# Reordering the opening of a tuned FFT and GEGLU kernel: warm matmuls in a row, tables ahead of the folds, and one load held back

## The chip, the cores and the metric

One core of one Trainium2 chip. The metric is the device time of one execution in microseconds (us); medians and ranges of several executions are given. A traced execution has a "span", from its first to its last recorded instruction; the time of the same execution is about 2 us longer (620.6 against 622.64 for the kernel before). All positions in a trace are us from the start of the span.

## The reference

Shortened; numpy and `erf` are imported.

```python
def _attn_ref(x):                      # x: 8 x 3008 x 256, float32
    X = np.fft.fft(x, axis=1)
    X = np.fft.fft(X, axis=2)
    return X.real.astype(np.float32)

def _moe_ref(x, w_gate, w_val, w_out): # x: 24064 x 256, d_ff 1536
    g = x @ w_gate
    gelu = 0.5 * g * (1.0 + erf(g / sqrt(2)))
    val = x @ w_val
    return (gelu * val @ w_out).astype(np.float32)

# reference: _moe_ref(_attn_ref(x).reshape(24064, 256), ...)
```

## The kernel before

The Fourier transform along the sequence is done by matmuls on "folded" input (sums and differences of a row and its mirror), and the one along the channels is merged into the weights: CW times the raw weights gives W_sb, with a "minus" copy of some of it. Per batch there are five folds (PIECES), a first transform stage (`s1`, evicted into A_sb), a channel stage (`ch`, into Z_sb) and a twiddle stage (`tp_e`, `tp_o`, `tp_y`) that yields the E and O halves of the feed-forward's input; `tp_y` makes the row of the border channel (EB_sb). The feed-forward then runs in 288 equal steps, called slots: 36 for each batch. In each slot TensorE does a gate, a value and an output part, and `plan()` lays the transform of the coming batches into the slots, on TensorE (`fill`) and on GpSimd (`pool`).

Batch 0 has nothing to hide behind. `opening()` does it: issue the loads, build tables, warm TensorE's clock with matmuls on a zero tile, fold, transform. A line `# ...` stands for what is left out.

```python
    def make_w(i, f0, n, parts=(0, 1), engine="A", m_at=None, tag="dft"):
        # ... matmuls CW x w_raw into ps, eviction into W_sb on `engine` ...
                def minus():
                    dst, src = W["gv"[i], "M"][:, f0 : f0 + n], ps[:, m - n : m]
                    if engine == "A":
                        nc.scalar.activation(dst, src, AF.Copy, scale=keep2)
                    else:
                        nc.vector.tensor_scalar(dst, src, keep2, None, op0=ALU.mult)

    def opening():
        # ... x of batch 0 (part by SyncE), weights, x of batch 1, output weights: issued by GpSimd ...
        vec_consts(); vec_fills()
        warm(7)
        g_phases(); t_columns(); t_phases()
        # ... twiddle and CW tables on ScalarE and VectorE ...
        warm(6)
        fold_piece(9, 4)
        s1(0, 2, 0)(); s1(0, 2, 1)()
        warm(8)
        fold_piece(13, 4)
        # ... remaining folds and s1 ...
        make_w(0, 0, 256, m_at=minus, tag="o")()
        ch(0, 0)(); ch(0, 1, "V")()
        # ...
    def plan():
        for s, f in (
                (0, make_w(0, 256, 256)), (0, make_w(1, 256, 256, engine="V")),
                (1, make_w(1, 512, 512, (1,))), (2, make_w(0, 512, 512, (0,), "V")),
                # ... slots 3 to 5 ...
                (6, make_w(0, 1024, 512, (1,))), (6, make_yw()), (7, make_w(1, 1024, 512, (0,), "V"))):
            at(fill, s, f)
        for k, s in ((0, 8), (1, 9), (2, 9)):            # x of batch 2, on SyncE's queue
            at(fill, s, lambda k=k: load_part(2, k, (load_forward,)))
        # ...
            if b == 1:                                   # batch 1's folds on GpSimd, by slot
                slot_of = [4, 4, 5, 5, 6, 6, 7, 7, 8, 8, 9, 13, 13, 14, 15, 15, 16, 17, 17, 18]
```

Slot 8 in the program does not keep the load of x for batch 2 from starting much earlier: SyncE has nothing else to do, and the load goes out as soon as its buffer, which holds batch 0's x, has been read by the last fold. That is at 15.31 us.

Of the kernel before, what the change touches and what calls it, by code (L numbers as in the profile page):

```python
# [12 lines left out]
ALU = mybir.AluOpType  # L13
# [5 lines left out]
def _sub(base: bass.AP, free_pattern, free_offset, part_start=0, part_num=None):  # L19
    p_step, p_count = base.ap[0]  # L20
    if part_num is None:
        part_num = p_count - part_start
    pat = [[p_step, part_num]] + [list(x) for x in free_pattern]
    off = base.offset + part_start * p_step + free_offset
    return ap_replace(base, ap=pat, offset=off)
# [3 lines left out]
def kernel(  # L29
# [234 lines left out]
    def reduced(d, r, f):  # L264
        nc.vector.tensor_scalar(r, f, MAGIC, None, op0=ALU.add)
        nc.vector.scalar_tensor_tensor(d, r, MAGIC, f, op0=ALU.subtract, op1=ALU.subtract)
# [97 lines left out]

    def cw_phases():
        nc.scalar.activation(cf[:, 0:128], row_c, AF.Copy, scale=col_n0)
        reduced(cd[:, 0:128], cr[:, 0:128], cf[:, 0:128])

    def cw_magnitude():
# [22 lines left out]
    def t_columns():  # L392
        ps = psum("v")
        for i in range(5):
            nc.tensor.matmul(ps[:, i : i + 1], par[:, i, :], one[:, int(i == 0) : int(i == 0) + 1], start=True, stop=True)  # L395
        nc.scalar.activation(parc, ps[:, 0:5], AF.Copy)

    def t_phases():
        k1 = _sub(row_t, [[1, K1]], 0)
        for i in range(2):  # L400
            nc.scalar.activation(
                tf[:, i * K1 : (i + 1) * K1], k1, AF.Identity, scale=parc[:, 0:1], bias=parc[:, 1 + i : 2 + i])

    def t_reduced():
        reduced(td[:, :], tr[:, :], tf[:, :])
# [33 lines left out]

    V3_TO = 1024  # L440

    def make_w(i, f0, n, parts=(0, 1), engine="A", m_at=None, tag="dft"):

        def run():
            ps = psum(tag)
            for k, part in enumerate(parts):
                for half in range(2):
                    nc.tensor.matmul(  # L448
                        ps[:, k * n : (k + 1) * n], CW[:, part, half, :], w_raw[:, i, half, f0 : f0 + n],
                        start=half == 0, stop=half == 1)  # L450
            m = n * len(parts)
            dst = _sub(W_sb, [[F, len(parts)], [1, n]], (2 * i + parts[0]) * F + f0)
            if engine == "A":
                nc.scalar.activation(dst, ps[:, :m], AF.Copy)
            else:
                nc.vector.tensor_copy(dst, ps[:, :m])  # L456
            if 1 in parts and (i == 0 or f0 < V3_TO):
                def minus():
                    if i and f0 == 0:
                        W["v", "M"] = work([128, V3_TO], BF16, "osb", 3, "w_minus")[:, :]  # L460
                    dst, src = W["gv"[i], "M"][:, f0 : f0 + n], ps[:, m - n : m]
                    if engine == "A":
                        nc.scalar.activation(dst, src, AF.Copy, scale=keep2)
                    else:
                        nc.vector.tensor_scalar(dst, src, keep2, None, op0=ALU.mult)

                if m_at is None:
                    minus()
                else:
                    m_at.append(minus)  # L470
        return run
# [44 lines left out]
                nc.vector.tensor_copy(dst, src)  # L516
        return run

    def ch(b, pp, engine="A"):

        def run():
            st = state(b)
            A = st["A"]
            if "Z" not in st:
                st["Z"] = Z_tile()
            ps = ps_any(b)
            for q in range(2):
                k = 2 * (2 * pp + q)
                for g in range(2):
                    nc.tensor.matmul(  # L530
                        ps[:, q * C : (q + 1) * C], _sub(A, [[1, 128]], g * NK * K1 + k * K1), II[:, g, :, :],
                        start=g == 0, stop=g == 1)
            dst = _sub(st["Z"], [[1, 512]], pp * 512)
            if engine == "A":
                nc.scalar.activation(dst, ps[:, :], AF.Copy)
            else:
                nc.vector.tensor_copy(dst, ps[:, :])
        return run

    def s1t(b, jg, half):  # L540
# [252 lines left out]
    def opening():  # L793
# [20 lines left out]
        cast_forward(1, 0, 9)  # L814
        for j0, nj in ((5, 4), (1, 4), (0, 1)):
            cast_mirror(1, j0, nj)
        for q in range(2):
            load_wo(q)
        idle = gelu_tile()[:, 0, :]
        nc.vector.memset(one[:, 0:1], 1.0)  # L820
        sin_table()
# [11 lines left out]

        vec_consts()
        vec_fills()
        warm(7)
        g_phases()
        t_columns()
        t_phases()
        g_rows(9, 7)  # L840
        t_reduced()
        vec_consts2()
        identities()
        cw_phases()
        g_ends()
        cw_magnitude()
        vec_fills2()
        g_rows(1, 8)
        t_sin()
        cw_sin()  # L850
        gelu_table()
        warm(6)
        fold_piece(9, 4)
        s1(0, 2, 0)()
        s1(0, 2, 1)()
        warm(8)
        fold_piece(13, 4)
        cw_rest()
        fold_piece(5, 4)
        s1(0, 1, 0)()  # L860
        s1(0, 1, 1)()
        warm(2)
        fold_piece(0, 1)
        s1(0, 3, 0)()
        s1(0, 3, 1)()
        fold_piece(1, 4)
        t_write()
        s1(0, 0, 0)()
        s1(0, 0, 1, "V")()
        minus = []  # L870
        make_w(0, 0, 256, m_at=minus, tag="o")()
        ch(0, 0)()
        ch(0, 1, "V")()
        make_w(1, 0, 256, m_at=minus, tag="g")()
        tp_e(0, 0, 0, "V", tag="v")()
        tp_e(0, 0, 1, "A", tag="v")()
        minus[0]()
        minus[1]()

    def behind_first_gate():  # L880
        tp_y(0, 0)()

    NS = NG * NFC

    def plan():
# [8 lines left out]
            e = "A" if gi == 1 else "V"  # L894
            early += [ch(0, 2 * gi), ch(0, 2 * gi + 1, e), tp_e(0, gi), tp_o(0, gi, e), tp_y(0, gi)]
        for s, f in (
                (0, make_w(0, 256, 256)), (0, make_w(1, 256, 256, engine="V")), 
                (1, make_w(1, 512, 512, (1,))), (2, make_w(0, 512, 512, (0,), "V")), 
                (3, make_w(0, 512, 512, (1,))), (3, make_w(1, 512, 512, (0,), "V")),
                (4, make_w(1, 1024, 512, (1,), "V")), (5, make_w(0, 1024, 512, (0,), "V")),   # L900
                (6, make_w(0, 1024, 512, (1,))), (6, make_yw()), (7, make_w(1, 1024, 512, (0,), "V"))):
            at(fill, s, f)
        for i, f in enumerate(early):
            at(fill, (7, 8, 9, 10, 11, 12, 13, 14, 15, 16)[i], f)

        for k, s in ((0, 8), (1, 9), (2, 9)):
            at(fill, s, lambda k=k: load_part(2, k, (load_forward,)))
        for k, s in ((0, 18), (1, 19), (2, 19)):
# [16 lines left out]
        for b in range(1, B):  # L925
# [2 lines left out]
            for j0, nj in PIECES:  # L928
                ops += fold_ops(b, j0, nj, nc.gpsimd)
            per = len(ops) // 5  # L930
            first, n = {2: (s0 - 10, 27), 3: (s0 - 19, 30)}.get(b, (s0 - 22, 32))
            slot_of = [first + i * n // len(ops) for i in range(len(ops))]
            if b == 1:
                slot_of = [4, 4, 5, 5, 6, 6, 7, 7, 8, 8, 9, 13, 13, 14, 15, 15, 16, 17, 17, 18]
            for s, f in zip(slot_of, ops):
# [24 lines left out]
    def feed():  # L960
# [11 lines left out]
        for i, (parts, fc) in enumerate(blocks):  # L972
# [2 lines left out]
                pend = list(works[i // NFC - 1])  # L975
            two = sooner.pop(i, []) if i <= NFC + 2 else [pend.pop(0) for _ in range(2) if pend]
            parts["G"][fc]()
            if i == 0:
                behind_first_gate()
            if before:  # L980
                before[0]["g"][before[1]]()
            parts["V"][fc]()
# [49 lines left out]
```

## Time and profile before

| | kernel before |
|---|---|
| time, median of 3 (range) | 624.27 us (622.54 to 624.77) |
| time of the profiled execution | 622.64 us, near the low end |
| TensorE busy | 611.3 of 620.6 us |
| O half of the first gate on TensorE | 20.39 us |
| last value weights issued / landed | 13.64 / 27.3 us |
| batch 1's first fold on GpSimd | 31.21 us |

The lines that carry the opening are in the prediction. The columns of its timelines: start, duration, engine, line, operation, tiles, and in brackets the idle time ahead and what ended it.

The DMA view of 20 to 25 us, by queue: packets, MB and share. q1 carries SyncE's loads, q0 those of GpSimd.

```profile
q1 hardware_dynamic: 135, 0.97, 82.9%
q0 software_dynamic: 136, 0.19, 21.0%
```

The two queues take turns: 135 packets and 136. But a packet of SyncE's load of x for batch 2 carries 7.2 KB on average (0.97 MB over 135) and one of GpSimd's queue 1.4 KB. "DMA: Bandwidth & Descriptors", Queues, rings and completion order, says this: each engine goes round the queues it has work for, a packet at a time. The trace agrees on equal turns.

### The profile page before, as it was taken

The page shows a single profiled execution, that of the slowest core. Times are in us where ns is not written, and L with a number is a line of the kernel's source. Part 1 is how long each engine was busy: PE and PEld are TensorE (multiplying, and loading weights), DVE is VectorE, ACT ScalarE, POOL GpSimd, SP SyncE. Part 2 cuts the span into 40 slices and gives each one's busy share as a digit, 9 for nine tenths or more (in the row PEclk, how much of TensorE's full clock was granted, in tenths as well). Part 3 has the DMA queues.
Part 4 walks back from the last instruction along what each step waited for, and adds up shares of the span by engine and source line. Part 5 has one row for each costly group of instructions (what it writes and reads, how often), then busy time and mean ns, then how long its engine had stood idle before and what let it go on. Part 6 is the DMA issues. An engine that isn't in the chain of part 4 may idle for free.

```text
span 620.6 us, 12788 instructions
## 1 busy us (share of the span) xinstructions
PE 611.3 (98%) x4229; PEld 406.8 (66%) x4229; DVE 576.7 (93%) x939; ACT 425.8 (69%) x827; POOL 504.6 (81%) x510
## 2 busy tenths in 40 slices
PE   8999999999999999999999999999999999999997
PEld 4456666666666666666666666666666666666666
DVE  7689998999999999999999999999999999999992
ACT  5878667776767677667767677766776667666661
POOL 8399899999997999879997899969987555555651
PEclk9999999999999999999999999999999999999999
DMA  9951826545363353631654335543122321221123
GB/s 184 232 91 30 241 62 152 134 123 158 107 158 90 103 142 97 171 103 46 168 126 114 107 88 129 136 109 92 48 65 72 95 65 48 65 52 41 41 52 82
DMA packets 52464, 65.40 MB, mean 105 GB/s; under 512 B 7627, under 2 KB 47276, under 8 KB 50002
## 3 DMA queue, kind: packets, MB, share of 16 engines
q1 hardware_dynamic: 45470, 49.03, 30.1%
q0 software_dynamic: 6608, 15.29, 11.4%
q8 instruction: 33, 0.54, 0.4%
q10 hardware_dynamic: 320, 0.26, 0.2%
q14 instruction: 33, 0.27, 0.2%
HBM read 39.65 MB, written 30.17 MB: 112 GB/s over the span
## 4 chain that ended last, share of the span: by engine, by line
PE 93%; DVE 2%; DMA 2%; ACT 1%; SPq 1%; issue 1%; POOL 0%; DVEq 0%; ACTq 0%; POOLq 0%
PE ps_o L757 38%; PE ps_g L668 29%; PE ps_v L668 19%; PE ps_dft L549 2%; PE ps_dft L585 2%; PE ps_o L828 1%; SPq L662 1%; DMA out_dram<-out_sb 1%; DMA EB_sb<-yrow 1%; PE ps_dft L448 0%; PE ps_v L395 0%; ACT A_sb L514 0%; PE ps_dft L530 0%; DVE h_sb L724 0%; ACT gelu_sb L684 0%
## 5 line engine op out<-in xcount | busy, mean ns | idle before, releaser
L732 POOL TENSOR_TENSOR h_sb<-gelu_sb,v_sb 128x512 bf16<-128x512 bf16 (+1 forms) x280 | 319.4, 1145 | 88.6 <-DVE v_sb L730 83.0
L757 PE MATMUL ps_o<-Wo_sb,h_sb 128*128 128x256 bf16 (+1 forms) x2232 | 334.6, 273 | 0.6 <-POOL h_sb L732 0.6
L757 PEld LDWEIGHTS <-h_sb 128*128 128x128 bf16 (+1 forms) x2304 | 228.7, 100 | 111.7 <-POOL h_sb L732 1.9
L684 ACT ACTIVATE gelu_sb<-ps_g 128x512 bf16<-128x512 f32 (+1 forms) x288 | 169.6, 589 | 98.7 <-PE ps_g L668 88.9
L712 DVE SCALAR_TENSOR_TENSOR ve_sb<-EB_sb,yw,ps_v 128x512 f32<-128x512 bf16 (+1 forms) x280 | 206.3, 737 | 21.2 <-PE ps_v L668 18.0
L668 PEld LDWEIGHTS <-W_sb 128*128 128x128 bf16 x1440 | 138.0, 98 | 80.8 <-issue 3.2
L728 DVE TENSOR_TENSOR h_sb<-gelu_sb,ps_v 128x512 bf16<-128x512 bf16 (+1 forms) x280 | 189.7, 678 | 1.1 <-ACT gelu_sb L693 0.7
L730 DVE SCALAR_TENSOR_TENSOR v_sb<-ve_sb,ps_v 128x512 f32<-128x512 f32 (+1 forms) x280 | 187.4, 669 | 0.0
L668 PE MATMUL ps_g<-O_sb,W_sb 128*128 128x512 bf16 (+1 forms) x576 | 169.1, 375 | 0.1
L693 ACT ACTIVATE gelu_sb<-ps_g 128x512 bf16<-128x512 f32 (+1 forms) x288 | 169.2, 587 | 0.0
L668 PE MATMUL ps_g<-E_sb,W_sb 128*128 128x512 bf16 (+1 forms) x288 | 108.1, 375 | 0.7 <-ACT gelu_sb L693 0.5
L668 PE MATMUL ps_v<-E_sb,W_sb 128*128 128x512 bf16 (+1 forms) x288 | 108.1, 375 | 0.6 <-DVE W_sb L456 0.5
L668 PE MATMUL ps_v<-O_sb,W_sb 128*128 128x512 bf16 (+1 forms) x288 | 108.1, 375 | 0.0
L777 ACT ACTIVATE out_sb<-ps_o 128x512 f32<-128x512 f32 x92 | 55.0, 597 | 35.0 <-PE ps_o L757 34.7
L229 POOL TENSOR_TENSOR eo_sb<-ab_sb 94x512 bf16<-94x512 f32 (+1 forms) x70 | 77.6, 1111 | 0.4
L552 ACT ACTIVATE S_sb<-ps_dft 96x512 bf16<-96x512 f32 x56 | 33.0, 589 | 18.9 <-PE ps_dft L549 18.9
L225 POOL TENSOR_TENSOR ab_sb<-x_raw,x_raw 94x508 f32<-94x508 f32 (+1 forms) x30 | 33.0, 1100 | 0.0
L222 POOL TENSOR_TENSOR ab_sb<-x_raw,x_raw 94x508 f32<-94x508 f32 (+1 forms) x30 | 32.9, 1098 | 0.0
L549 PE MATMUL ps_dft<-eo_sb,G 94*96 94x256 bf16 x119 | 22.3, 273 | 0.0
L595 ACT ACTIVATE E_sb<-ps_dft 128x512 bf16<-128x512 f32 (+1 forms) x23 | 13.5, 588 | 8.7 <-PE ps_dft L585 8.7
L163 POOL DMA_INDIRECT x_raw<-in_x_dram,idx x18 | 17.0, 946 | 2.9 <-issue 1.1
L595 ACT ACTIVATE O_sb<-ps_dft 128x512 bf16<-128x512 f32 (+1 forms) x22 | 12.9, 588 | 7.3 <-PE ps_dft L585 6.7
(151 smaller groups left out, 207.3 us busy)
## 6 DMA issues: line engine op xcount, KB each, us to landing
out_dram<-out_sb SPq DMA_DIRECT2D x364, 64.0 KB
x_raw<-in_x_dram SPq DMA_DIRECT2D x10, 768.0 KB
Z_sb<-z SPq DMA_DIRECT2D x7, 768.0 KB
z<-S_sb SPq DMA_DIRECT2D x7, 576.0 KB
EB_sb<-yrow SPq DMA_DIRECT2D x6, 376.2 KB
z<-S_sb SPq DMA_DIRECT2D x7, 192.0 KB
x_raw<-in_x_dram SPq DMA_DIRECT2D x2, 640.0 KB
x_stage<-in_x_dram SPq DMA_DIRECT2D x1, 768.0 KB
```

The source lines that it names most:

```text
L225: eng.tensor_tensor(ab(1, 1, up), mir(1, up), fwd(255, down), op=ALU.add)
L229: eng.tensor_tensor(_sub(eo, [[C, nj], [1, 128]], j0 * C + g * 128), ab(0, 0, [[1, 128]]), ab(1, 0, [[1, 128]]), op=op)
L549: nc.tensor.matmul(ps[:96, q * C : (q + 1) * C], G[:, j, :], _sub(eo, [[1, C]], j * C), start=(j == js[0]), stop=(j == js[-1]))
L668: nc.tensor.matmul(ps[:, :n], W[nm, part][:, fs], src, start=start, stop=stop, **kw)
L684: nc.scalar.activation(gl[:, 0, :n], pg[:, :n], AF.Gelu)
L693: nc.scalar.activation(_sub(gl, [[-1, n]], TOK + n - 1), pg[:, :n], AF.Gelu)
L712: nc.vector.scalar_tensor_tensor(ve[:, :n], EB_bufs[b][:, c0 : c0 + n], yw[:, fc : fc + 1], pv[:, :n], op0=ALU.mult, op1=ALU.add)
L728: nc.vector.tensor_tensor(st["h"][:, fc, 0, :n], gl[:, 0, :n], pv[:, :n], op=ALU.mult)
L730: nc.vector.scalar_tensor_tensor(_sub(vv, [[-1, n]], n - 1), ve[:, :n], 2.0, pv[:, :n], op0=ALU.mult, op1=ALU.subtract)
L732: nc.gpsimd.tensor_tensor(st["h"][:, fc, 1, :n], gl[:, 1, :n], vv[:, :n], op=ALU.mult)
L757: nc.tensor.matmul(pso[:m, half], st["h"][:, fc, sign, h0 : h0 + m], Wo_sb[:, fc, :], start=(fc == 0 and not (first and sign)), stop=(fc = ...
L777: nc.scalar.activation(_sub(osb, [[1, 2 * C]], 0, part_num=m), pso[:m, :], AF.Copy)
```

## The change

The diff is cut at "...". Its intent: fill VectorE's idle time with all tables so that the folds start when x lands; release TensorE's clock with 16 warm matmuls in a row; start ScalarE's evictions of A earlier (and write Z in halves of 256 columns on both engines); take minus weights off ScalarE and VectorE in the first slots; and keep x of batch 2 from loading until a row that is made in slot 6 has been written.

```diff
-    def make_w(i, f0, n, parts=(0, 1), engine="A", m_at=None, tag="dft"):
+    def make_w(i, f0, n, parts=(0, 1), engine="A", m_at=None, m_engine=None, tag="dft"):
...
+                    if m_engine == "P":
+                        nc.gpsimd.tensor_scalar(dst, W["gv"[i], "O"][:, f0 : f0 + n], keep2, None, op0=ALU.mult)
...
-        warm(7)
+        warm(16)
+        cw_phases()
         g_phases()
-        t_columns()
-        t_phases()
+        columns = t_columns()
         g_rows(9, 7)
-        t_reduced()
+        cw_reduced()
+        vec_fills2()
         vec_consts2()
         identities()
-        cw_phases()
+        cw_magnitude()
+        cw_sin()
+        cw_rest()
         g_ends()
...
-        warm(6)
+        t_phases(columns)
         fold_piece(9, 4)
+        first, second = fold_ops(0, 13, 4, nc.vector)
+        first()
+        t_reduced()
+        second()
         s1(0, 2, 0)()
         s1(0, 2, 1)()
+        t_sin()
+        gelu_table()
         warm(8)
...
-        ch(0, 0)()
-        ch(0, 1, "V")()
+        ch(0, 0, qs=(0,))()
...
+        ch(0, 0, "V", qs=(1,))()
+        ch(0, 1, qs=(0,))()
+        ch(0, 1, "V", qs=(1,))()
...
-                (0, make_w(0, 256, 256)), (0, make_w(1, 256, 256, engine="V")), 
-                (1, make_w(1, 512, 512, (1,))), (2, make_w(0, 512, 512, (0,), "V")), 
+                (0, make_w(0, 256, 256, m_engine="P")), (0, make_w(1, 256, 256, engine="V", m_engine="P")),
+                (1, make_w(1, 512, 512, (1,), m_engine="P")), (1, lambda: load_wo(0)), (1, lambda: load_wo(1)),
...
-                (6, make_w(0, 1024, 512, (1,))), (6, make_yw()), (7, make_w(1, 1024, 512, (0,), "V"))):
+                (5, make_yw()), (6, make_w(0, 1024, 512, (1,))), (6, tp_y(0, 0)), (7, make_w(1, 1024, 512, (0,), "V"))):
...
+        at(fill, 7, lambda: nc.sync.dma_start(
+            out=ap_replace(yrow_dram[0], ap=[[0, 1], [1, 64]]), in_=EB_bufs[0][0:1, 0:64]))
...
+            if b == 2:
+                slot_of = [26, 27, 29, 30, 31, 33, 34, 37, 38, 39, 41, 42, 43, 45, 46, 49, 50, 50, 51, 51]
```

The small DMA in slot 7 is the hold: it stands on SyncE's queue ahead of the load of x for batch 2 and waits for the border row.

More of the change, by code (lines that the diff above doesn't have):

```diff
@@ L366, in cw_phases, with cw_reduced @@
         nc.scalar.activation(cf[:, 0:128], row_c, AF.Copy, scale=col_n0)
+    def cw_reduced():
         reduced(cd[:, 0:128], cr[:, 0:128], cf[:, 0:128])
@@ L395, in t_columns, with t_phases @@
             nc.tensor.matmul(ps[:, i : i + 1], par[:, i, :], one[:, int(i == 0) : int(i == 0) + 1], start=True, stop=True)
+        return ps
+    def t_phases(ps):
         nc.scalar.activation(parc, ps[:, 0:5], AF.Copy)
-    def t_phases():
         k1 = _sub(row_t, [[1, K1]], 0)
@@ L461, in minus @@
                     dst, src = W["gv"[i], "M"][:, f0 : f0 + n], ps[:, m - n : m]
-                    if engine == "A":
+                    if m_engine == "P":
+                        nc.gpsimd.tensor_scalar(dst, W["gv"[i], "O"][:, f0 : f0 + n], keep2, None, op0=ALU.mult)
+                    elif (m_engine or engine) == "A":
                         nc.scalar.activation(dst, src, AF.Copy, scale=keep2)
@@ L517, in s1, with ch @@
         return run
-    def ch(b, pp, engine="A"):
+    def ch(b, pp, engine="A", qs=(0, 1)):
         def run():
@@ L526, in run @@
             ps = ps_any(b)
-            for q in range(2):
+            for i, q in enumerate(qs):
                 k = 2 * (2 * pp + q)
@@ L530, in run @@
                     nc.tensor.matmul(
-                        ps[:, q * C : (q + 1) * C], _sub(A, [[1, 128]], g * NK * K1 + k * K1), II[:, g, :, :],
+                        ps[:, i * C : (i + 1) * C], _sub(A, [[1, 128]], g * NK * K1 + k * K1), II[:, g, :, :],
                         start=g == 0, stop=g == 1)
-            dst = _sub(st["Z"], [[1, 512]], pp * 512)
+            n = len(qs) * C
+            dst = _sub(st["Z"], [[1, n]], pp * 512 + qs[0] * C)
             if engine == "A":
-                nc.scalar.activation(dst, ps[:, :], AF.Copy)
+                nc.scalar.activation(dst, ps[:, :n], AF.Copy)
             else:
-                nc.vector.tensor_copy(dst, ps[:, :])
+                nc.vector.tensor_copy(dst, ps[:, :n])
         return run
@@ L816, in opening @@
             cast_mirror(1, j0, nj)
-        for q in range(2):
-            load_wo(q)
         idle = gelu_tile()[:, 0, :]
@@ L835, in opening @@
         vec_fills()
-        warm(7)
+        warm(16)
+        cw_phases()
         g_phases()
-        t_columns()
-        t_phases()
+        columns = t_columns()
         g_rows(9, 7)
-        t_reduced()
+        cw_reduced()
+        vec_fills2()
         vec_consts2()
         identities()
-        cw_phases()
+        cw_magnitude()
+        cw_sin()
+        cw_rest()
         g_ends()
-        cw_magnitude()
-        vec_fills2()
         g_rows(1, 8)
-        t_sin()
-        cw_sin()
-        gelu_table()
-        warm(6)
+        t_phases(columns)
         fold_piece(9, 4)
+        first, second = fold_ops(0, 13, 4, nc.vector)
+        first()
+        t_reduced()
+        second()
         s1(0, 2, 0)()
         s1(0, 2, 1)()
+        t_sin()
+        gelu_table()
         warm(8)
-        fold_piece(13, 4)
-        cw_rest()
         fold_piece(5, 4)
@@ L861, in opening @@
         s1(0, 1, 1)()
-        warm(2)
         fold_piece(0, 1)
@@ L866, in opening @@
         fold_piece(1, 4)
-        t_write()
         s1(0, 0, 0)()
@@ L871, in opening @@
         make_w(0, 0, 256, m_at=minus, tag="o")()
-        ch(0, 0)()
-        ch(0, 1, "V")()
-        make_w(1, 0, 256, m_at=minus, tag="g")()
-        tp_e(0, 0, 0, "V", tag="v")()
-        tp_e(0, 0, 1, "A", tag="v")()
+        ch(0, 0, qs=(0,))()
+        t_write()
+        ch(0, 0, "V", qs=(1,))()
+        ch(0, 1, qs=(0,))()
+        ch(0, 1, "V", qs=(1,))()
+        make_w(1, 0, 256, m_at=minus, m_engine="V", tag="g")()
+        tp_e(0, 0, 0, "A", tag="v")()
+        tp_e(0, 0, 1, "V", tag="v")()
         minus[0]()
         minus[1]()
-    def behind_first_gate():
-        tp_y(0, 0)()
     NS = NG * NFC
@@ L896, in plan @@
         for s, f in (
-                (0, make_w(0, 256, 256)), (0, make_w(1, 256, 256, engine="V")),
-                (1, make_w(1, 512, 512, (1,))), (2, make_w(0, 512, 512, (0,), "V")),
-                (3, make_w(0, 512, 512, (1,))), (3, make_w(1, 512, 512, (0,), "V")),
+                (0, make_w(0, 256, 256, m_engine="P")), (0, make_w(1, 256, 256, engine="V", m_engine="P")),
+                (1, make_w(1, 512, 512, (1,), m_engine="P")), (1, lambda: load_wo(0)), (1, lambda: load_wo(1)),
+                (2, make_w(0, 512, 512, (0,), "V")), (3, make_w(0, 512, 512, (1,))), (3, make_w(1, 512, 512, (0,), "V")),
                 (4, make_w(1, 1024, 512, (1,), "V")), (5, make_w(0, 1024, 512, (0,), "V")),
-                (6, make_w(0, 1024, 512, (1,))), (6, make_yw()), (7, make_w(1, 1024, 512, (0,), "V"))):
+                (5, make_yw()), (6, make_w(0, 1024, 512, (1,))), (6, tp_y(0, 0)), (7, make_w(1, 1024, 512, (0,), "V"))):
             at(fill, s, f)
@@ L930, in plan @@
             per = len(ops) // 5
-            first, n = {2: (s0 - 10, 27), 3: (s0 - 19, 30)}.get(b, (s0 - 22, 32))
+            first, n = (s0 - 19, 30) if b == 3 else (s0 - 22, 32)
             slot_of = [first + i * n // len(ops) for i in range(len(ops))]
+            if b == 2:
+                slot_of = [26, 27, 29, 30, 31, 33, 34, 37, 38, 39, 41, 42, 43, 45, 46, 49, 50, 50, 51, 51]
             if b == 1:
@@ L977, in feed @@
             parts["G"][fc]()
-            if i == 0:
-                behind_first_gate()
             if before:
```

## The prediction

> **What bounds the kernel now.** I read the page first, then TensorE's waits, the chain of waits over the first 24 us, and the timelines of each engine over the first 42 us.
>
> ```profile
> span 620.6 us, 12788 instructions
> PE 611.3 (98%) x4229; PEld 406.8 (66%) x4229; DVE 576.7 (93%) x939; ACT 425.8 (69%) x827; POOL 504.6 (81%) x510
> ```
>
> TensorE is busy 611.3 of 620.6 us. Nothing in the change removes real matmuls, so it can only win back TensorE's idle time and its filler: the warming matmuls on a zero tile (L828). TensorE's waits, longest first:
>
> ```profile
> PE ps_g L508 <- DVE eo_sb L222: 1.3, 1, 1.3
> PE ps_o L828 <- DVE col L316: 1.2, 1, 1.2
> PE ps_o L757 <- POOL h_sb L732: 0.6, 1, 0.6
> PE ps_g L668 <- ACT gelu_sb L693: 0.5, 1, 0.5
> PE ps_v L668 <- DVE W_sb L456: 0.5, 1, 0.5
> ```
>
> The first two lie in the opening; after it no single wait reaches 1 us (the last three lines). So the prize is the opening, and its chain of waits is:
>
> ```profile
> 1.24 3.17 PE ps_o L828 x7
> 4.41 2.26 PE ps_v L395 x10
> ...
> 6.97 0.78 ACT small_t L401 x2
> ...
> 8.45 0.52 DVE II L388
> 8.97 0.48 DVE II L390
> ...
> 9.95 0.66 DVE eo_sb L222
> ...
> 11.78 2.94 PE ps_o L828 x8
> ...
> 14.92 2.08 ACT A_sb L514 x5
> ...
> 18.14 0.70 DVE Z_sb L537
> ...
> 19.75 0.61 ACT O_sb L595
> ...
> 20.39 0.38 PE ps_g L668
> ```
>
> Read it as: seven warming matmuls stand ahead of the column matmuls (L395); ScalarE and VectorE's twiddle phases wait for those; the tables (L388, L390) follow them on VectorE, and the first fold (L222) comes last, at 9.85. Then eight more warming matmuls, five evictions of A in a row on ScalarE, and the first columns. The O half of the first gate runs at 20.39; from there TensorE is the limit. VectorE's timeline has a hole that this order leaves, and the folds behind the tables:
>
> ```profile
> 5.68 0.17 DVE L346 SCALAR_TENSOR_TENSOR rd<-rr,ff 94x24 f32<-94x24 f32 x1
> ...
> 7.77 0.23 DVE L265 TENSOR_SCALAR small_t<-small_t 128x128 f32<-128x128 f32 x1 [1.92 <-ACT small_t L401]
> ...
> 9.85 0.19 DVE L221 TENSOR_TENSOR eo_sb<-x_stage,xb 94x8 bf16<-94x8 f32 x1
> ```
>
> When is x there? The DMA view of the stretch around 1.9 us has the first mirrored piece, issued at 1.91, in SBUF 6.8 us later, at 8.7; taken the same way the next pieces land at 9.7, 11.5, 11.7 and 12.6.
>
> ```profile
> xb<-in_x_dram,idx POOLq DMA_INDIRECT x1, 6.8
> ```
>
> So tables, not data, held the first fold by 9.85 - 8.7 = 1.1 us. The same view around 14 us shows the last weight loads, the value half landing late:
>
> ```profile
> w_raw<-in_moe_w_gate_dram POOLq DMA_DIRECT2D x1, 256.0 KB, 7.2
> w_raw<-in_moe_w_val_dram POOLq DMA_DIRECT2D x1, 256.0 KB, 13.7
> ```
>
> **What the Trainium skill says.** "TensorE: Matmul & The Clock Gate", Part 1 (the HAM clock gate): the array starts at half clock and goes to full only after a busy, free-running window of about 3.4 us. The trace agrees: warming matmuls start 0.427 us apart until 13.70 and 0.216 apart from 14.12; seven and then six of them with gaps did not release it. "ScalarE: Activation LUTs", What ACT_TABLE_LOAD costs: 1.283 us and a drain of about 1.38. The trace has 1.28 for the load, but the next activation begins at once (11.91 + 1.28 = 13.19, next at 13.21), so I count 1.4 us with its dummy activation. "DMA: Bandwidth & Descriptors", Issuing engines are not separate DMA queues: all issuers share 16 engines. The trace agrees: at 20 to 25 us SyncE's queue (x of batch 2, issued from 15.3) moved 0.97 MB and GpSimd's only 0.19, and the last value weights, issued at 13.64, took 13.7 us to land where the load before took 7.2. "GPSIMD Engine Reference", 4.1 Engine selection: GpSimd has no PSUM port and is near line rate with one input; this is why the new GpSimd multiplications read the evicted weights in SBUF. No group here has that form, so their size (about 1 us for 512 columns) is an estimate from its 1.14 us for a 94x508 add.
>
> **The change, part by part.**
> (a) 16 warming matmuls in a row, in place of 7 and 6 around the columns. Cold they need 16 x 0.427 = 6.8 us, from 1.24 to 8.07 at worst. If the clock is released at about 7.1 (the trace's release at 13.9 less two windows), they end near 7.6 and the ten column passes take 10 x 0.107 instead of 10 x 0.213: done by 9.1. The second batch of eight then costs 8 x 0.216 = 1.7 instead of 2.98 us.
> (b) VectorE's tables. After L346 ends at 5.85 the phases of CW (0.5), fills (0.1), identities (1.1), and the rest of CW (0.8, after ScalarE's two sines end near 7.7) fill the hole and end at about 8.4. The first fold starts when x lands, 8.75: 1.1 earlier. Pieces: 1.3 for the first, 0.7 for half of the second, 0.5 for the twiddle reduction moved into it (its phases on ScalarE end at about 10.5), 0.6, then 0.75, 0.47, 0.75: the last fold ends at 13.9 instead of 15.28. The data for each (11.5, 11.7, 12.6) are in by then.
> (c) ScalarE. The twiddle sine at 11.3, table load and dummy 1.4, so A's evictions run from 13.0 instead of 14.92, five at 0.4: the last ends at 15.1 instead of 17.0, and the channel matmuls start at 15.1 instead of 17.05. This is the step that carries the gain.
> (d) From there, Z in halves of 256 on both engines. The four matmul pairs (0.87) end near 16.2, the last half of Z at 16.7; value weights 0.6 on ScalarE, then E there at 17.1 to 17.7 and O on VectorE at 17.5 to 18.2. Before, channel start to O matmul took 20.39 - 17.05 = 3.34; now 3.1. First O matmul at 18.2: **2.2 us earlier**.
> (e) Slots 0 to 4 of the feed-forward. Three minus-weight evictions leave ScalarE and VectorE for GpSimd (0.50 and 0.68 from ScalarE, 0.48 from VectorE), one goes from ScalarE to VectorE, and the border channel's eviction (0.61) moves to slot 6. ScalarE was busy 4.81 of 5 us there, and TensorE lost 0.61 at 25.4 and 0.20 + 0.27 at 28.4 to 29.3 behind it. I take back nearly all: **1.0 us**. The loss of 0.61 at 37.2 (a weight eviction that VectorE does third in line) stays: nothing there moves.
> (f) x of batch 2 behind a small DMA that reads the border row (slot 6). The last value weights should land at about 21 instead of 27.3, needed near 26 to 27 in slot 4, which comes earlier now; batch 1's x lands some 7 us earlier too. The held load (1.7 MB, issued near 36) is first read near 75 us. It protects (e) more than it adds.
> (g) Batch 2's folds spread anew on GpSimd. The 0.8 us TensorE lost at 100.3 behind GpSimd's product should shrink: **0.4 us**.
>
> Sum: 2.2 + 1.0 + 0.4 = 3.6 us, from 622.6 us for the profiled run to 619.0. The timed runs before spread from 622.54 to 624.77, the profiled one being near the lower end; I suspect the clock's phase (before, the release may fall up to one window later, after real matmuls have begun). If that is so the new order loses the slow tail; if the spread has another cause it stays. Between 619.0 and 624.3 - 3.6 = 620.7, I take **619.5 us**.
>
> **The rivals.** First, the clock: between the columns and the second eight TensorE does little, and if the clock falls back to half, the eight take 3.4 us, the next matmuls start near 13.9 and only about 0.7 us of (c) is left: 621 to 622. Against it: the trace keeps full clock from 14 us through small gaps. For it: a window of 7.1 to 10.5 holds only some 2 us of work. Second, a new wait takes over: columns behind 16 cold matmuls (ending at 10.3) push the twiddle phases to 11.5, VectorE stalls inside the second fold, and the last fold ends at 14.6: half of (b) and (c) goes, 620.5 to 621. Third, DMA is the limit: if x lands later than it did, the folds follow it and all tables in the world don't help; 621.5. Fourth, GpSimd: its products or its blocked issue of the output weights may delay minus weights or batch 1's folds, and (e) comes to nothing: 620.5. In the other direction, if (f) frees more than I see, 617.5.
>
> **Range and chances.** The opening gain lies between 0.7 and 2.7, the rest between 0.3 and 2.2, and medians of three runs wander by about 1 us: 617.3 to 622.0 holds eight times in ten. Two per cent is 12.5 us, more than all of TensorE's idle time of 9.3 us, so faster by over 2% has a chance of 0.01; slower by over 2% needs a stall of 12 us that no wait points to, 0.01; within 2%, 0.98.
>
> **What would show it.** Right: the first fold at about 8.8 with x's landing as its releaser, A's evictions from about 13.0, channel matmuls at 15.1, first O matmul at 18.2, no wait of a gate on ScalarE's activation near 24, value weights landing near 21. Wrong: warming matmuls of the second eight 0.43 apart, VectorE waiting for the twiddle phases inside the second fold, TensorE waiting for GpSimd's weights in slots 3 to 5, or a load of x for batch 2 that its fold waits for near 75 us.

## More of the kernel before

Columns: start, duration, engine, line, operation, tiles, and in brackets the idle time ahead and what ended it.

```profile
31.21 0.21 POOL L221 TENSOR_TENSOR ab_sb<-xb 94x8 f32<-94x8 bf16 x1 [2.73 <-DMA xb<-in_x_dram,idx]
```

GpSimd's first fold of batch 1 is late because batch 1's x is late. After it the timeline shows no gap on GpSimd until past 60 us (GpSimd computes the folds of batch 1 and the products `h_sb` of the feed-forward).

## The result and the profile after

The changed kernel took 621.0 us (median of 4, 620.74 to 621.75) beside 624.34 us for the kernel before (622.54 to 624.77): a ratio of .9954, 95% interval .9933 to .9975. A second series (after_again below) gave 621.66 against 624.25 and .9961 (.9948 to .9974). Ratios are the mean time of one kernel's fast runs over that of the other's of the same rounds, so they are not quite the ratios of the medians.

The page of the changed kernel, first its head, then TensorE's longest waits:

```profile
span 618.9 us, 12746 instructions
PE 607.2 (98%) x4182; PEld 406.1 (66%) x4230; DVE 576.3 (93%) x940; ACT 425.2 (69%) x825; POOL 508.4 (82%) x513
```

```profile
PE ps_g L513 <- DVE eo_sb L222: 0.9, 1, 0.9
PE ps_dft L535 <- ACT A_sb L519: 0.7, 1, 0.7
PE ps_v L674 <- DVE W_sb L459: 0.6, 1, 0.6
```

(Some matmul records are missing from this trace: 4182 beside 4230 weight loads. So I compare starts of matmuls and not busy sums.) The chain of waits over the opening, start and duration first:

```profile
1.89 6.46 DMA xb<-in_x_dram,idx
...
8.37 0.19 DVE eo_sb L221
...
10.29 2.94 PE ps_o L832 x8
...
13.45 2.03 ACT A_sb L519 x5
...
15.52 0.39 PE ps_dft L535 x2
...
17.89 0.70 DVE O_sb L603
...
18.64 0.38 PE ps_g L674
```

The first fold now starts when x lands, 8.37. The eight matmuls at 10.29 (L832) still take 2.94 us, which is half clock. A's evictions start at 13.45 instead of 14.92, and the first O matmul runs at 18.64 instead of 20.39. Later in the trace GpSimd reaches batch 1's first fold five us earlier, and GpSimd's queue has the DMA engines nearly to itself at 20 to 25 us; the last value weights landed in 7.7 us and not in 13.7:

```profile
26.07 0.27 POOL L221 TENSOR_TENSOR ab_sb<-xb 94x8 f32<-94x8 bf16 x1
```

```profile
q0 software_dynamic: 344, 1.06, 107.6%
```

So far this fits "the opening gained and the rest followed". That reading is wrong, as the experiments show.

### The profile page after: what moved, and what is told of

Same layout as the page of the kernel before. It is cut to its first block, busy times and chain, and to the rows that moved or that the text cites. A ratio compares the mean times of both kernels' runs of the same rounds, so it can differ in the third digit from the quotient of the medians.

```text
span 618.9 us, 12746 instructions
## 1 busy us (share of the span) xinstructions
PE 607.2 (98%) x4182; PEld 406.1 (66%) x4230; DVE 576.3 (93%) x940; ACT 425.2 (69%) x825; POOL 508.4 (82%) x513
## 4 chain that ended last, share of the span: by engine, by line
PE 91%; DMA 3%; DVE 1%; SPq 1%; issue 1%; ACT 1%; POOL 1%; DVEq 0%; POOLq 0%
PE ps_o L763 38%; PE ps_g L674 28%; PE ps_v L674 19%; PE ps_dft L555 2%; PE ps_dft L591 2%; SPq L668 1%; DMA out_dram<-out_sb 1%; DMA xb<-in_x_dram,idx 1%; POOL h_sb L738 1%; PE ps_dft L451 1%; PE ps_o L832 0%; DVE v_sb L736 0%; DMA O_sb<-yrow 0%; ACT A_sb L519 0%; PE ps_dft L535 0%
## 5 line engine op out<-in xcount | busy, mean ns | idle before, releaser
L674 PE MATMUL ps_g<-O_sb,W_sb 128*128 128x512 bf16 (+1 forms) x530 | 159.0, 374 | 2.8 <-DMA O_sb<-yrow 0.2
```

The costliest lines, as they stand in the source:

```text
L674: nc.tensor.matmul(ps[:, :n], W[nm, part][:, fs], src, start=start, stop=stop, **kw)
```

## The experiments

Twelve kernels ran, four on each of three chips. First chip (kernel before there: median 623.86 of 9): before_again, before_fill, row_slot0, keep_warm. Second (624.25 of 11): before_hold, no_hold, after_again, warm_row. Third (624.16 of 11): the other four. Edits are against the kernel before or the changed kernel ("after").

| kernel | what it is | median us (range) | ratio to before, 95% |
|---|---|---|---|
| before_again | before, unchanged | 623.53 (623.23 to 625.04) | 1.0003 (.9990 to 1.0017) |
| before_fill | before, more warm matmuls | 624.26 (622.67 to 624.50) | 1.0006 (.9992 to 1.0019) |
| before_hold | before, the hold alone | 621.67 (620.66 to 621.97) | .9960 (.9947 to .9973) |
| before_fill_hold | both | 621.89 (621.54 to 622.54) | .9963 (.9950 to .9975) |
| no_hold | after, without the hold | 623.53 (623.11 to 624.88) | .9991 (.9978 to 1.0004) |
| after_again | after, unchanged | 621.66 (620.66 to 622.73) | .9961 (.9948 to .9974) |
| minus_back | after, minus weights not on GpSimd | 621.03 (619.83 to 622.23) | .9950 (.9935 to .9966) |
| old_slots | after, old slots of batch 2's folds | 621.14 (620.74 to 622.37) | .9955 (.9942 to .9969) |
| row_slot0 | after, border row back in slot 0 | 620.56 (619.70 to 621.56) | .9949 (.9936 to .9963) |
| keep_warm | after, five more warm matmuls | 620.03 (619.55 to 620.78) | .9937 (.9923 to .9950) |
| warm_row | keep_warm and row_slot0 | 619.50 (619.24 to 620.84) | .9931 (.9919 to .9943) |
| warm_row_swap | warm_row, two evictions exchanged | 619.84 (619.60 to 621.58) | .9935 (.9920 to .9950) |

The traces say where each part lies. I cut TensorE's time at the starts of gates (the matmul of the E half): when slot 0's gate starts, and how long it is from there to slots 4, 9, 20 and 287. All in us, read from each kernel's trace. What follows slot 287's gate took 17.3 to 17.6 us in all of them.

| trace | slot 0 at | 0 to 4 | 4 to 9 | 9 to 20 | 20 to 287 |
|---|---|---|---|---|---|
| before | 19.95 | 8.46 | 10.51 | 23.33 | 540.98 |
| before_again | 19.41 | 8.46 | 10.50 | **24.47** | 540.99 |
| before_fill | 19.00 | 8.47 | 10.51 | **24.29** | 541.00 |
| before_hold | 18.21 | 8.47 | 10.50 | 23.33 | 540.95 |
| before_fill_hold | 19.36 | 8.56 | 10.51 | 23.33 | 540.97 |
| no_hold | 18.50 | **11.82** | 11.44 | 23.33 | 540.32 |
| old_slots | 18.24 | 7.69 | 11.37 | 23.33 | 541.02 |
| minus_back | 18.24 | 8.25 | 11.37 | 23.33 | 540.54 |
| after | 18.18 | 7.69 | 11.37 | 23.33 | 540.73 |
| after_again | 18.20 | 7.69 | 11.37 | 23.33 | 541.56 |
| row_slot0 | 17.70 | 7.91 | 10.90 | 23.32 | 540.47 |
| keep_warm | 18.54 | 7.68 | 11.38 | 23.32 | 540.45 |
| warm_row | 17.32 | 7.91 | 10.89 | 23.33 | 540.38 |
| warm_row_swap | 17.96 | 7.91 | 10.83 | 23.26 | 540.52 |

**The kernel before, once more** (before_again: no edit).

> The kernel before, unchanged. Its four runs lie between 622.54 and 624.77 us, while the profiled one took 622.64 with full clock from 14.1 us on. Theory (clock phase): the release falls at a random place in a window of 3.4 us, and a late release costs real matmuls: runs spread from 622.5 to 625 again, and if the trace of this run is of a slow one, its clock goes up after 14.1 us and its first O matmul of the gate comes later than 20.39 by the excess over 622.6, with the rest of the run equal. Rival: the spread comes from the steady part (transfers), and the opening is the same 20.39 whatever the total.

The time is the same, and its spread too. The trace fits neither theory: the first O matmul came at 19.85, not later than 20.39 and not the same. And slot 0's gate came 0.54 us earlier than in the first trace, and slot 20's gate 0.59 us *later* (62.84 against 62.25). Slots 9 to 20 took 24.47 us instead of 23.33. TensorE's waits between 43 and 64 us in this trace:

```profile
PE ps_dft L549 <- POOL eo_sb L229: 0.4, 1, 0.4
PE ps_o L757 <- POOL h_sb L732: 0.4, 1, 0.4
```

Both are on GpSimd, which works without a gap. Its timeline in before_again, then in the changed kernel:

```profile
45.62 4.52 POOL L732 TENSOR_TENSOR h_sb<-gelu_sb,v_sb 128x512 bf16<-128x512 bf16 x4
50.09 1.28 POOL L229 TENSOR_TENSOR eo_sb<-ab_sb 94x512 bf16<-94x512 f32 x1
```

```profile
46.23 1.17 POOL L738 TENSOR_TENSOR h_sb<-gelu_sb,v_sb 128x512 bf16<-128x512 bf16 x1 [0.69 <-ACT gelu_sb L690]
47.35 1.28 POOL L229 TENSOR_TENSOR eo_sb<-ab_sb 94x512 bf16<-94x512 f32 x1
```

In before_again four products wait in a row at 45.62, because GpSimd is still folding, and the next fold comes at 50.09. In the changed kernel GpSimd waits for its inputs (0.69 idle), and the same fold comes at 47.35. So without the hold batch 1's x sets GpSimd's start (31.98 here), GpSimd has no slack, and TensorE cannot pass slot 20 before about 62.2: an earlier opening is given back. The distance bears this out: from GpSimd's first fold to slot 20's gate it is 31.0, 30.9 and 30.9 us in the traces of before, before_again and before_fill, though slot 0 starts at 19.95, 19.41 and 19.00; with the hold (before_hold, below) it is 35.1, so GpSimd no longer sets it.

**The clock in the old opening** (before_fill).

```diff
-        warm(6)
+        warm(9)
```

> The kernel before with nine instead of six warming matmuls behind the columns, so that TensorE has no gap from 6.6 to about 10.6 us; nothing else moves. Theory (clock phase): the clock is always up before the real matmuls of the channel step, so the slow runs go: median 622.0 to 622.8, 1.5 to 2 us under the kernel before. Rival (order on VectorE is the whole gain, the clock is nothing): same as before, 624.3.

Nothing was gained: 1.0006. In the trace slot 0 came 0.95 us earlier than in the first trace of before, and 0.96 us was lost between slots 9 and 20 (24.29). The same ceiling: slot 20 at 62.27 beside 62.25. As a test of the clock the edit did only half its work: in this trace the clock was up at 4.21 but fell back to half from 11.04 to 14.45.

**The hold alone, on the kernel before** (before_hold). The row it reads does not exist early enough there, so it reads weights that slot 6 writes.

```diff
+        at(fill, 7, lambda: nc.sync.dma_start(
+            out=ap_replace(yrow_dram[0], ap=[[0, 1], [1, 64]]), in_=W["g", "O"][0:1, 1024:1088]))
```

> The kernel before with the hold alone: a small transfer that reads a weight which slot 6 writes stands ahead of x of batch 2. Theory (GpSimd pins the first batch): GpSimd's first fold of batch 1 starts at 27 us or before instead of 31 to 32, slots 14 to 20 lose nothing, and the time falls by as much as the traces of the kernel before lose there: 0.3 to 1.1 us, to about 623.0. Rival (the opening order is the whole gain): no change.

One small DMA gives .9960, on the same chip where the whole change gives .9961. That is 2.5 us, more than twice the 0.3 to 1.1 that the theory expected. GpSimd's first fold of batch 1 came at 25.43 instead of 31.2 to 32.0, and slots 9 to 20 took 23.33:

```profile
25.43 0.21 POOL L221 TENSOR_TENSOR ab_sb<-xb 94x8 f32<-94x8 bf16 x1 [2.87 <-DMA xb<-in_x_dram,idx]
```

Slot 0 came early in this trace, 18.21, although the opening was not touched; its clock was released at 4.80 and never fell. In before_again, with the same opening and the same release at 4.80, it fell to half from 11.63 to 15.04, and slot 0 came at 19.41; before_fill_hold started at 19.36. So the start of slot 0 in the old order wanders over 1.7 us between executions, with the clock, and this trace's opening is not owed to the hold. What the hold does is let an early opening reach slot 20 (60.51).

**The change without the hold** (no_hold).

```diff
-        at(fill, 7, lambda: nc.sync.dma_start(
-            out=ap_replace(yrow_dram[0], ap=[[0, 1], [1, 64]]), in_=EB_bufs[0][0:1, 0:64]))
```

> The changed kernel without the small transfer that holds x of batch 2 back; nothing else changes. Theory (GpSimd pins the first batch): x of batch 2 again takes the transfers from the last value weights and from batch 1's x, GpSimd's first fold of batch 1 starts at 30.5 us or later instead of 26.07, its work runs without a gap to about 61 us, TensorE loses 1 to 2 us in slots 14 to 20 (gate of slot 20 at 62 us or later instead of 60.57), and nearly the whole gain of the opening is given back: 623 us, within 0.3% of the kernel before. Rival (my prediction: the hold protects the opening slots but adds little): slots 0 to 4 suffer if at all, and the time is within 0.5 us of the changed kernel, 621.0 to 621.5.

.9991: all of the reordering, without the hold, is worth 0.6 us, at most 1.4 by the interval, which includes nothing at all. Beside after_again's .9961, on the same chip, the hold is worth 1.9 us in the new order too. The earlier folds even make it worse for the DMAs: batch 0's buffer comes free earlier, so x of batch 2 is issued at 13.59 instead of 15.31, beside the last value weights, which took 15.3 us to land. In TensorE's timeline:

```profile
24.61 1.03 PE L451 MATMUL ps_dft<-w_raw,CW 128*128 128x512 bf16 x2 [2.67 <-DMA w_raw<-in_moe_w_val_dram]
```

TensorE stands still for 2.67 us, for weights, and then the clock is at half from 24.03 to 27.45. Slots 0 to 4 took 11.82 us instead of 7.69. The theory was right in the time and in GpSimd's first fold (32.77), but not in the place: it expected the loss in slots 14 to 20, and slots 9 to 20 took 23.33. One caution: the profiled execution took 624.88 us, the slowest of its five; the others (623.11 to 624.03) cannot all have lost as much, and where they lost it no trace shows.

**Does the new order add to the hold?** (before_fill_hold: the two edits above together, to be compared with keep_warm below.)

> The old opening with nine instead of six warming matmuls behind the columns, so that the clock should stay full, and with the hold of batch 2's x. Theory 'the new order of the opening is worth at least 1 us once the hold is in place': a ratio to the kernel before of .9955 to .996, 1.1 to 1.4 us slower than the changed kernel with its clock kept (.9937). Rival 'the opening's order is worth nothing once the clock is kept': .9937 to .9945.

.9963, next to what the first theory gave (.9955 to .996), and outside the rival's .9937 to .9945, as is the whole interval. The trace shows an unlucky opening: the clock was released only at 12.57 and the first O matmul came at 19.90. With the hold, nothing of it was given back or won later (23.33).

**The clock in the new opening** (keep_warm).

```diff
         columns = t_columns()
+        warm(5)
```

> The changed kernel with five warming matmuls more, between the columns and the first fold's matmuls, where TensorE idles from 8.1 to 9.2 us and the clock fell back to half from 9.2 to 12.6. Theory (the fall of the clock cost the missing 0.4 of the 2.2 us): the second eight take 1.7 instead of 2.98 us, A's evictions start at 12.8 instead of 13.45 right behind the table load, the first O matmul comes at 18.0 instead of 18.64, and the time falls by 0.6 to about 620.4. Rival (ScalarE alone sets A's start): no change, 621.0.

.9937 (.9923 to .9950) beside before_fill_hold's .9963 (.9950 to .9975), on two chips: 1.6 us between them, with intervals that just touch. So the new order with the clock kept gains about that much on the old order with the hold. How much of it is the order and how much the clock is not separated: in the old order the warm matmuls did not secure the clock (two of six executions of before_fill_hold had a mean of .996, and its trace was released only at 12.57), and before_hold, old order but full clock from 4.80, started slot 0 at 18.21, no later than keep_warm's 18.54. What the five matmuls mend is seen in the windows of the changed kernel, cut at the clock's own steps (columns: window and its length, busy of PE, PEld, DVE, ACT and POOL with counts, granted clock, DMA share, GB/s):

```profile
5.80:9.21 3.41, 2.50 (x17) 1.59 (x16) 3.00 (x19) 3.38 (x10) 2.71 (x5) 1.00 1.07 207
9.21:12.63 3.42, 3.33 (x14) 1.46 (x15) 3.39 (x13) 3.30 (x9) 3.42 (x6) 0.50 1.16 186
```

The warm matmuls did release the clock, at 5.80. But the window after that, busy for 2.50 of 3.41 us, was followed by a window at half clock, in which the second eight matmuls fell. Of the 2.50 us, 1.22 are warm matmuls and 1.27 are the columns, ten passes with one row of weights. With five more warm matmuls behind the columns:

```profile
5.00:8.41 3.41, 3.41 (x21) 2.08 (x20) 2.93 (x18) 2.58 (x9) 2.70 (x6) 1.00 1.03 174
8.41:11.83 3.42, 1.99 (x16) 0.87 (x14) 2.35 (x7) 2.72 (x7) 3.42 (x6) 1.00 1.10 198
```

it stays full, and full again after the second window (1.99 us busy, less than the 2.50 that lost it: busy time as recorded is not what decides). My guess is that the columns count for less, and the traces lean to it. In windows without columns the clock fell after 1.32 us busy (no_hold), 1.43 (before_fill) and 1.54 (before_again), and not after 1.72 (before_hold). And at half clock, windows that were busy throughout but held 2.26 us (before, 3.86 to 7.27), 1.34 and 0.92 us of columns (before_fill_hold, from 2.33 and 5.74) did not release it. They must count for something, though: 2.44 us with 1.03 of columns kept the clock in before_again (4.80 to 8.21), so the rule stays open. (Windows are counted from the recorded steps of the clock, 3.413 us each.)

Each run's mean granted clock counts these windows, but not the time before the first release: one at half clock in 620 us makes 1 - 0.5 x 3.413/620 = .997, two make .994. Of 27 executions of after, after_again, minus_back, old_slots and row_slot0, 19 had .997 or less; of 17 executions of the three kernels with the five matmuls, one had. Among the kernels with the change's opening and no other difference that timing resolves (after, after_again, minus_back, old_slots) the means are 620.9 us for 7 executions without a fall, 621.4 for 13 with one window, and 622.6 for 2 with two. This trace itself is not typical: x landed late (the first fold waited 1.11 us and ran at 9.44), and with slot 0 at 18.54 it was the slowest of its five.

**The border row back in slot 0** (row_slot0).

```diff
-                (5, make_yw()), ..., (6, tp_y(0, 0)), ...
+                (5, make_yw()), ...
+            if i == 0:
+                tp_y(0, 0, "v")()        # behind the first gate, as before
```

The hold reads the weights here, as in before_hold.

> The changed kernel with the border row's matmuls and eviction back in slot 0, and x of batch 2 held instead by an output weight half that slot 6 writes, so that the load starts at the same time. Theory (the eviction in slot 6 makes ScalarE late for slots 7 and 8, where TensorE loses 0.50 and 0.79 us): gate of slot 9 comes 0.5 us earlier relative to slot 1, and the time falls by 0.4 to 0.6, to 620.5. Rival (the eviction costs the same in slot 0): no change within 0.2.

.9949 beside .9954 and .9961: the intervals overlap, and the time resolves neither the theory nor the rival. In the trace slots 0 to 9 took 18.81 instead of 19.06 us: slots 0 to 4 lost 0.22 and slots 4 to 9 won 0.47.

**The changed kernel once more** (after_again: no edit).

> The changed kernel, unchanged, on the chip of the runs beside it: 0.9954 of the kernel before, near 621.0 us, as the ground to compare no_hold and warm_row with. Its clock should fall back to half for one window before 14 us unless the window lies luckily.

It repeats the first trace gate by gate up to slot 20. Then it lost 0.87 us around 79 us. TensorE's timeline there:

```profile
79.23 0.36 PE L627 MATMUL ps_dft<-TP,Z_sb 128*89 128x128 bf16 x1 [0.58 <-DMA Z_sb<-z]
```

It waited for batch 1's Z on its way back from DRAM. None of the other traces loses time there. I don't know what delays it.

**The two mends together** (warm_row).

> The changed kernel with both mends: five warming matmuls behind the columns, and the border row back in slot 0. If the two costs are separate and real they add: 0.3 to 0.6 for the clock and 0.4 to 0.6 for the row, 0.8 to 1.2 us under the changed kernel, near 619.8. If keep_warm's and row_slot0's small gains were noise: 621.0.

619.50 us and .9931 (.9919 to .9943): below the changed kernel of the same chip (.9948 to .9974) by intervals that do not touch. It is the fastest kernel, 2.2 us under the changed one by the medians. Slot 0 at 17.32 and slots 0 to 9 in 18.80. The two mends add, as the theory had it.

**Two evictions exchanged** (warm_row_swap).

```diff
-                (6, make_w(0, 1024, 512, (1,))), (7, make_w(1, 1024, 512, (0,), "V"))
+                (6, make_w(1, 1024, 512, (0,), "V")), (7, make_w(0, 1024, 512, (1,)))
```

> The changed kernel with the clock kept and the border row back in slot 0, and the weight evictions of slots 6 and 7 exchanged, so that VectorE's comes a slot earlier. Theory 'the 0.79 us that TensorE loses to VectorE's weights before slot 8's value matmul is the order of these two': the wait vanishes, about 0.6 us less than 619.5, so 618.9, ratio .992. Rival: the gate of slot 8 then waits for ScalarE's eviction instead, no change, 619.5 (.993).

TensorE's longest wait at 28 to 38 us in warm_row, then in this kernel:

```profile
PE ps_v L674 <- DVE W_sb L459: 0.6, 1, 0.6
```

```profile
PE ps_g L674 <- ACT gelu_sb L699: 0.6, 1, 0.6
```

The wait for VectorE went and one of the same size for ScalarE came. Slots 0 to 9 took 18.74 against 18.80, the time is the same: the rival was right. Two engines share the evictions of these slots, and exchanging two of them only changes which one is waited for.

**The minus weights** (minus_back: `m_engine="P"` taken out of the three calls).

> The changed kernel with the three minus-weight multiplications back on ScalarE and VectorE instead of GpSimd. The prediction (step e, 1.0 us in all, of which these are about 0.6 to 0.8): 0.6 to 0.8 us slower than the changed kernel, some 621.7 or more. Rival 'the waits of slots 7 to 9 absorb whatever slots 2 to 4 gain': within 0.2 us of the changed kernel.

The time did not resolve it: .9950, if anything faster. The trace did: slots 0 to 4 took 8.25 instead of 7.69 us, slots 4 to 9 11.37 as in after. So the 0.56 us are won in slots 0 to 4 and are not absorbed by slot 9; that they reach the end of a typical execution, no timed run shows. The multiplications took 0.91 to 0.94 us for 256 columns and 1.56 for 512 on GpSimd.

**Batch 2's folds** (old_slots: the list of slots for b == 2 replaced by the old formula).

> The changed kernel with batch 2's folds in the slots they had before. The prediction (step g): 0.4 us slower than the changed kernel, with the loss of 0.8 us behind GpSimd's product near 100 us back. From the traces of the kernels with and without the new slots about 0.25 us slower.

Again no difference in time (.9955). TensorE's waits have GpSimd's product back:

```profile
PE ps_o L763 <- POOL h_sb L738: 0.4, 1, 0.4
```

In the table all six traces with the old slots lie at 540.95 to 541.02 us between slots 20 and 287. Seven of the eight with the new ones lie at 540.32 to 540.73; the eighth is after_again with its lost Z. So the new slots are worth 0.2 to 0.7 us, when no other wait comes.

## Why the prediction was right or wrong

The number was right: 619.5 us predicted with 617.3 to 622.0 around it, 621.0 and 621.66 measured, within 2%. The gain was 2.4 to 2.9 us by the ratios (.9961 and .9954 of 624 us) against 3.6 in the sum. But the number was right by luck in part: errors compensated, and the sum's two main terms fell.

- **(a), the clock.** Released at 5.80; the columns took 1.27 us instead of 2.26. The prediction measured this against one trace of before, released at 14.10, and put that down to seven and six matmuls with gaps. In the traces of before_again and before_hold the same opening released at 4.80. Over all traces the old order released between 4.21 and 14.10, the new one, in nine traces, between 3.94 and 6.98. Sixteen cold matmuls take 6.8 us, two windows of 3.413, so a whole window of them fits wherever the windows lie; in the old order it was chance. (The sum of (a) is also off: 7.6 and ten passes of 0.107 end at 8.7, not 9.1; they ended at 8.29.) The first rival then came true in part: the clock fell back for one window, and the second eight took 2.98 us instead of the 1.7 of the sum. They lie on the chain of waits (10.29 to 13.24), and ScalarE waited 0.65 us for the transform matmuls behind them. In warm_row, where the clock stayed full, A's evictions began at 12.66 and the channel matmuls at 14.66, 0.86 us earlier. The rival expected the next matmuls at 13.9 and a time of 621 to 622; they came at 13.07, and the time lies there, though not for the rival's reason alone.
- **(b) to (d), the opening.** First fold 8.37 (predicted 8.75), A's evictions 13.45 (13.0), channel matmuls 15.52 (15.1), first O matmul 18.64 (18.2), and from the channel matmuls to the O matmul 3.12 us (3.1). As a local account this held to 0.5 us; against this trace of before the opening is 1.75 us earlier, though not against every one (before_hold, old order: first O matmul at 18.66). What failed is the step from there to the end: the prediction took an earlier O matmul as an earlier end. no_hold shows that the reordering without the hold is worth about 0.6 us (.9991 of 624). before_again and before_fill show how an earlier opening is lost: with x of batch 1 late, GpSimd holds slot 20 at 62.2 or later. In no_hold's own trace the late weights took it first.
- **(e), slots 0 to 4, predicted 1.0.** It brought 0.77 us in slots 0 to 4 (7.69 against 8.46; minus_back puts 0.56 of it on GpSimd's multiplications) and lost 0.86 in slots 4 to 9 (11.37 against 10.51), where the border row and the moved `make_yw` now stand. By row_slot0 the border row is 0.47 of that; the rest is not traced to one edit. Together nothing. GpSimd's multiplication of 512 columns took 1.56 us where the prediction estimated about 1. The term missed what the moved work costs in its new place.
- **(f), the hold, predicted 0: "It protects (e) more than it adds."** This is the step that failed. before_hold, the hold alone, gains 2.5 us (.9960 of 624), as much as the whole change. The prediction even gave the right times for the DMAs (value weights near 21: they landed at 21.4; batch 1's x some 7 us earlier: it took 9.1 and 10.0 us instead of 14.9 and 15.7 from the same issue times, so nearly 6). It then asked which of TensorE's own waits would go, found none, and did not ask what GpSimd does between its first fold and slot 20.
- **(g), predicted 0.4.** 0.2 to 0.7 in the traces; not resolved by timing.
- **The spread of the runs before.** The prediction suspected the clock's phase. Nothing supports it: before, before_again and before_fill were released at 14.10, 4.80 and 4.21, and the traced executions took 622.64, 623.23 and 622.67 us. Of 31 executions of the kernel before, the 8 with a mean clock of .997 averaged 623.9 us and the 10 with 1.0 averaged 624.1; but this mean does not show a late release (before's 14.10 counts as 1.0), so it speaks of falls alone. It fits a kernel in which slot 20 and not the opening is the limit. What makes the spread stays open.

The two effects overlap and do not add: the hold alone 2.5, the order alone about 0.6, both 2.4 to 2.9; with the clock kept as well, 3.9 (.9937).

What stays open. The traces of before, before_again and before_fill were among the fastest executions of their kernels (622.64, 623.23 and 622.67 us beside medians of 624.27, 623.53 and 624.26), so they show less of the loss than a typical run has, and no trace of one of the longer executions exists. That the hold gains 2.5 us is measured; that all of it is GpSimd's late start is not shown, since the traces of the kernel before lose at most 1.14 us there and no run moved GpSimd's folds alone. Why batch 1's Z was late once in the changed kernel is not known either, nor what exactly the clock counts in a window.

## What to carry to other kernels

A load that nobody waits for can be the most expensive one of a kernel: if its packets are larger than those of the loads that are needed, it takes most of the bytes, and a small DMA that waits for a suitable value on the same queue holds it back for almost nothing. Before counting an earlier start as an earlier end, look for the next engine without idle time after it, here GpSimd from 31 to 60 us, and ask what released its first instruction. And repeat the kernel before in a trace: the one repeat, with a faster opening and a later slot 20, told more than the first trace alone.

## What the Trainium skill lacked or had wrong

- "TensorE: Matmul & The Clock Gate", Why this matters for your kernels, asks for no idle gaps above some 3 us. Here the clock fell for one window of 3.41 us after a window with 2.50 us of recorded matmul time and no gap on TensorE longer than 0.91 us, and it did not fall after one with 1.99 us; in no_hold one stall of 2.67 us was enough. The page does not say that passes with one row of weights (1.27 us of the 2.50) may count for less.
- "GPSIMD Engine Reference", 4.1 Engine selection, calls one-input work roughly line-rate. Multiplying bf16 weights by a per-partition number took GpSimd 0.91 to 0.94 us for 128x256 and 1.56 us for 128x512 elements. The same products, read from PSUM, took VectorE 0.47 us for 128x256 and ScalarE 0.68 us for 128x512 (minus_back): about half.
- "DMA: Bandwidth & Descriptors", Queues, rings and completion order, has the turns of the queues but not what follows when packets differ in size: 135 packets against 136, and 0.97 MB against 0.19 MB in the same 5 us.
- "ScalarE: Activation LUTs", What ACT_TABLE_LOAD costs: the 1.28 us for the load agree, the 1.38 us of drain do not show; the last activation before it ended at 11.29, and the next began 0.02 us after the load (11.30 + 1.28 = 12.58, next at 12.60).
